# A new unit order for a Sinkhorn-sorted attention followed by a token-mixing MLP

## The chip, the cores and the metric

The kernel runs on one NeuronCore of a Trainium2 chip. The metric is the device time of one launch in microseconds (us), as the median of several runs. The engines are PE (matrix products, with its weight loads shown apart as PEld), VectorE (DVE), ScalarE (ACT), GpSimd (POOL) and SyncE (SP); each runs its own instructions in program order, and they meet through semaphores. Transfers (DMA) are started by GpSimd, SyncE or ScalarE.

## The reference

Four batches, eight heads, 768 tokens in eight blocks of 96, head size 64. Five Sinkhorn steps turn an 8x8 matrix per head into a nearly doubly stochastic P; P mixes the blocks of k and v; each block of q attends to its mixed block; the heads are joined to x (768 x 512 per batch), and a token-mixing MLP follows.

```python
for _ in range(5):
    P = exp(P - max(P, -1)); P = P / (sum(P, -1) + 1e-9); P = P / (sum(P, -2) + 1e-9)
k_sorted, v_sorted = einsum('bhij,bhjcd->bhicd', P, blocks of k), the same of v
attn = softmax(q_b @ k_sb.T / sqrt(64))          # per block of 96 tokens
x = (attn @ v_sb) joined over heads              # [4, 768, 512]
W_tok = (x @ w_q) @ (x @ w_k).T / sqrt(64)       # [768, 768] per batch
out = relu(W_tok @ x) @ w_out
```

## The kernel before

The work is cut into units, each a short function of a batch `b` and a number `n`. One table, `ORDER`, lists all 468 units, and the loop at the end issues them one after the other. Nothing else orders the work: an engine meets its instructions in the order in which their units stand in the table, and waits where a value or a buffer isn't ready. An item such as `K01:2` is unit `u_K` of batch 0, pair 1, with PSUM bank 2; `k01:A:2` is its copy out of that bank by engine A (ScalarE), D (VectorE), G (GpSimd) or S (SyncE, for transfers). Capital letters are PE work, apart from R, D and I, which are transfers.

What the units do, in the order of the data:

- `l..` loads. GpSimd starts the loads of k, v and q, each in two halves of four heads (`lk0a`, `lk0b`), with a cast from f32 to bf16 on the way (line L232; the MLP's weights L223 and L226). `I` brings the first batch's raw q by SyncE into the buffers XT (L268).
- `c` and `a` are the Sinkhorn steps, on VectorE and ScalarE in turn; they end with P's transpose (L197). `A` and `B` spread P over the partitions, `u` copies it to the tile PTR, and `n` builds the sorting matrices M (L253), for the first batch from PSUM, for the others from PTR.
- `Z` are idle products on the zero tile `fil`, `n` of them: nothing reads them.
- `z` (first batch) and `p` put a pair of heads of q side by side in a pair buffer; `z` casts from f32, `p` copies bf16 within SBUF. `Q` transposes the pair on PE, and `q` copies the result to QT.
- `K` and `Y` sort and turn k and v in one product against M, with copies `k`, `y` to KT. `F`, `f` turn the first batch's v back into VT; the other batches sort v with `V`, `v` into Vs, and six transfers `R` on SyncE (L330) bring it to VT.
- `S` scores, `e` exponential to E (L363), `P` weighted sum, `r` and `x` the division into X (L392).
- `T`, `t` transpose X on PE to XT for batches 0 and 1. For batches 2 and 3 the units `D` do it by two transposing transfers each on SyncE (L398).
- `J` projects to q and k of the MLP, `d` moves a half of it to other partitions (tile qD), `W`, `G`, `H` form the token mixing, `h` applies the relu, `O` multiplies by w_out, `o` copies to one of four output buffers `ot`, and `s` stores it (L485, for the last batch in parts at L488).

Every PE instruction stands on line L154; copies are on L158 (ScalarE), L160 (GpSimd) and L162 (VectorE). After the table a `guard` on GpSimd reduces the reciprocals (L500 and on) and branches to a slow path that isn't taken.

```python
    for item in ORDER.split():
        kind, arg = item[0], item.split(":")[1:]
        ...
        if kind.isupper() and kind not in "RNDI":
            fns[kind](b, n, int(arg[0]))
        else:
            fns[kind](b, n, arg[0], int(arg[1]) if len(arg) > 1 else None)
```

Of the kernel before, what the change touches and what calls it, by code (L numbers as in the profile page):

```python
# [19 lines left out]
ORDER = """  # L20
i00:G i02:D I00:S lk0b Z62:0 I01:S Z32:1 i03:G Z42:0 c00:D Z22:1 a01:A lk0a c01:D A00:0 Z52:1 lv0a
Z04:2 lv0b a02:A:0 c02:D lv1b Z12:0 lv1a z11:A lp z10:D a03:A Q01:0 c03:D Q00:1 q01:A:0 q00:A:1
a04:A c04:D z13:A lk1a z12:D a05:A Q03:1 c05:D q03:A:1 Q02:0 q02:A:0 lk1b B00:0 u00:A:0 n01:D:0
n10:G n03:D:0 K01:2 n02:D:0 Y01:4 n00:D:0 k01:A:2 lq1b K00:6 y01:A:4 S02:2 k00:D:6 n11:G Y02:0
e02:A:2 K02:4 y02:D:0 S01:6 lq1a e01:A:6 S00:2 F02:0 lo k02:A:4 F01:1 f02:D:0 Y00:6 e00:A:2 f01:D:1
S03:4 n20:G y00:D:6 K03:0 e03:A:4 V10:2 k03:D:0 lv2a F00:6 v10:A:2 V12:4 lk2a f00:D:6 S06:0 lv2b
R10:S S05:2 e06:A:0 v12:D:4 P01:6 e05:A:2 R11:S V11:0 lk2b r01:D:6 x01:D:6 R14:S K10:4 v11:A:0 K11:2
R15:S n30:G k11:A:2 S04:0 k10:D:4 R12:S P00:6 e04:A:0 R13:S K12:2 r00:D:6 x00:D:6 lq2a Y03:4 k12:A:2
P02:0 n21:G y03:A:4 r02:D:0 x02:D:0 T00:2 K13:6 t00:A:2 p12:G F03:4 p13:D T01:5 n31:G k13:A:6
f03:D:4 Q12:2 Q13:3 q12:D:2 P04:0 q13:A:3 P03:6 lq2b r04:D:0 x04:D:0 U00:4 S16:2 z01:A:4 r03:D:6  # L30
x03:D:6 S14:0 p10:G e16:A:2 U01:4 e14:A:0 S15:2 p11:G t01:D:5 T03:7 e15:A:2 z02:D:4 T02:6 t03:D:7
Q10:5 Q11:4 t02:A:6 q10:D:5 P13:2 lq3a q11:D:4 S10:0 r13:D:2 x13:D:2 S13:6 e10:A:0 S12:4 lv3b
e13:A:6 S11:0 J01:2 e12:A:4 J00:3 j01:D:2 lv3a P14:6 e11:A:0 j00:D:3 W01:2 d01:G P12:4 r14:D:6
x14:D:6 W00:2 d00:A P11:0 w00:A:2 r12:D:4 x12:D:4 lk3b K20:6 G00:2 k20:A:6 G01:2 r11:D:0 x11:D:0
T12:3 g00:A:2 T13:6 t12:A:3 lk3a V20:4 T11:7 t13:A:6 v20:D:4 H01:2 K21:0 h01:A:2 k21:D:0 lq3b R20:S
K23:4 K22:2 R21:S k23:D:4 V22:0 k22:A:2 O03:6 t11:D:7 v22:A:0 p21:G V21:2 o03:D:6 p20:G P10:4 R25:S
v21:A:2 Q21:0 r10:D:4 x10:D:4 R24:S H02:6 q21:A:0 p23:G H00:2 R23:S Q20:1 h02:A:6 p22:D R22:S T10:0
q20:D:1 Q22:4 Q23:5 t10:D:0 h00:A:2 S21:6 q23:D:5 J10:0 e21:A:6 q22:D:4 p31:G S20:2 j10:D:0 S23:4
e20:A:2 S26:6 p30:D J11:1 d10:G e26:A:6 Q30:0 j11:D:1 O00:2 e23:A:4 d11:D q30:D:0 W11:3 o00:A:2
S25:4 S24:0 e25:A:4 S22:6 O05:2 e24:A:0 O01:4 e22:A:6 P24:0 o01:D:4 O02:5 o05:A:2 r24:D:0 x24:D:0  # L40
s00:S P21:6 O04:2 o02:D:5 r21:D:6 x21:D:6 s01:S V30:0 o04:A:2 V32:4 v30:A:0 s02:S W10:3 Q31:2
v32:D:4 V31:6 w10:A:3 R30:S P23:0 v31:A:6 q31:D:2 R31:S K30:4 r23:D:0 x23:D:0 G10:3 R35:S k30:A:4
K31:6 G11:3 R32:S k31:A:6 K32:4 g10:D:3 R33:S P22:0 k32:A:4 p32:G S31:2 r22:D:0 x22:D:0 H12:6 R34:S
p33:G e31:A:2 H11:4 h12:A:6 h11:D:4 S32:2 D21:S Q32:0 Q33:1 e32:A:2 q32:D:0 H10:6 K33:4 q33:D:1
h10:A:6 S33:2 k33:D:4 P20:0 e33:A:2 O11:6 r20:D:0 x20:D:0 S34:2 o11:A:6 S35:4 O10:7 D20:S e35:A:4
P31:0 e34:A:2 o10:D:7 S36:4 O14:6 r31:D:0 x31:D:0 s10:G e36:A:4 P34:4 o14:A:6 P32:2 r34:D:4 x34:D:4
P33:0 S30:6 r33:D:0 x33:D:0 J21:4 e30:A:6 J20:5 j21:A:4 r32:D:2 x32:D:2 P30:0 j20:A:5 W21:4 W20:4
O12:5 d21:D w20:A:4 D31:S r30:D:0 x30:D:0 G20:4 o12:A:5 G21:4 d20:D D30:S O15:5 g20:A:4 H20:0
o15:D:5 H22:2 h20:A:0 H21:6 O13:4 s12:S h21:D:6 h22:A:2 O20:5 o13:D:4 O23:2 o20:A:5 s11:G J31:3
o23:D:2 J30:5 j31:D:3 O21:4 d31:D j30:A:5 d30:D W30:5 W31:5 o21:A:4 O25:3 w30:D:5 w31:A:5 s20:A  # L50
G31:2 o25:A:3 G30:2 O22:3 g30:A:2 H30:4 o22:D:3 H32:6 h30:A:4 H31:0 h32:D:6 O24:2 s21:S h31:A:0
O31:3 o24:D:2 O33:0 s22:S o31:A:3 s31:A O30:1 o33:D:0 O34:3 s33:S o30:D:1 O32:2 s30:S o34:D:3 O35:1
s34:S o32:A:2 s32:S o35:A:1 s35:S
"""


# [652 lines left out]
```

## Time and profile before

| | us |
|---|---|
| median of three runs | 102.31 |
| lowest and highest | 102.23, 105.89 |
| profiled execution | 102.0 |
| its span | 100.1 |
| PE busy | 86.0 |
| VectorE busy | 72.8 |
| ScalarE busy | 71.2 |
| GpSimd busy | 40.9 |

The span is the time between the first and the last instruction that the hardware profiler saw; the profiled execution took 1.9 us more than that. A row of the order of instructions reads: start, time, engine, line, operation, tile written and tiles read, shape, how many are merged, and in brackets how long the engine stood idle before and what ended it. Matrix products overlap one another, so the distance between two starts says more than the time beside them. The clock column is the share of its full speed that PE was granted.

### The profile page before, as it was taken

To read this page: it belongs to the slowest core of one execution; us is meant where nothing else is said; L and a number is where in the kernel's file an instruction comes from. 1 tells how busy PE (TensorE), PEld (TensorE's weight loads), DVE (VectorE), ACT (ScalarE), POOL (GpSimd) and SP (SyncE) were. 2 spreads that over 40 slices of the span, in tenths; PEclk is the share of its full clock that TensorE was granted. 3 is DMA by queue.
4 is the path that set the end of the run, shared out by engine and by line. 5 is a ranking of instruction groups with operands and counts; after the bars stand their busy time and mean duration, and the time that the engine had idled before them with its cause. 6 is when DMAs were issued, how large, how long until landed. Compare 5 with 4: busy or idle time off the path is not lost.

```text
span 100.1 us, 3190 instructions
## 1 busy us (share of the span) xinstructions
PE 86.0 (86%) x1332; PEld 59.6 (60%) x1332; DVE 72.8 (73%) x143; ACT 71.2 (71%) x100; POOL 40.9 (41%) x65
## 2 busy tenths in 40 slices
...
GB/s 14 278 342 219 203 203 203 200 203 202 219 248 248 212 202 205 202 209 197 227 236 248 214 269 416 263 98 194 58 184 131 181 220 229 110 213 213 360 354 124
DMA packets 24575, 21.39 MB, mean 214 GB/s; under 512 B 7280, under 2 KB 22640, under 8 KB 24560
## 3 DMA queue, kind: packets, MB, share of 16 engines
...
q14 instruction: 5, 0.04, 0.1%
...
## 4 chain that ended last, share of the span: by engine, by line
PE 51%; DMA 17%; DVE 14%; ACT 11%; issue 3%; SPq 0%; ACTq 0%; DVEq 0%
PE ps L154 51%; DMA VT<-Vs 8%; DMA XT<-X 5%; DMA XT<-in_q_dram 4%; DVE X L392 4%; ACT E L363 3%; ACT QT L158 2%; ACT Vs L158 2%; DVE Vs L162 1%; DVE mixT L462 1%; DVE QT L162 1%; DVE Rall L387 1%; DVE KT L162 1%; ACT Qn L158 1%; DVE VT L162 1%
## 5 line engine op out<-in xcount | busy, mean ns | idle before, releaser
L363 ACT ACTIVATE E<-ps 96x960 bf16<-96x960 f32 (+1 forms) x28 | 23.9, 900 | 2.7 <-PE ps L154 2.5
L154 PE MATMUL ps<-wo,mixT 128*128 128x512 bf16 x96 | 23.3, 380 | 0.0
L392 DVE TENSOR_TENSOR X<-ps,Rall 96x896 bf16<-96x896 f32 (+1 forms) x20 | 20.1, 1007 | 0.7
L162 DVE COPY ot<-ps 128x512 f32<-128x512 f32 x12 | 8.3, 690 | 10.6 <-PE ps L154 8.4
L154 PEld LDWEIGHTS <-mixT 128*128 128x128 bf16 x96 | 8.4, 98 | 9.0 <-issue 0.8
L158 ACT COPY ot<-ps 128x512 f32<-128x512 f32 (+1 forms) x13 | 7.6, 587 | 7.7 <-PE ps L154 7.1
L154 PEld LDWEIGHTS <-KT 64*128 64x128 bf16 (+1 forms) x288 | 8.8, 100 | 4.3 <-issue 3.0
L160 POOL COPY Qn<-Qn 128x768 bf16<-128x768 bf16 x9 | 7.3, 827 | 9.9 <-DMA Qn<-in_q_dram 9.9
L158 ACT CAST KT<-ps 128x768 bf16<-128x768 f32 x12 | 9.3, 800 | 2.5 <-PE ps L154 2.5
L154 PE MATMUL ps<-VT,E 96*128 96x65 bf16 x256 | 10.8, 193 | 0.3 <-DMA VT<-Vs 0.2
L154 PEld LDWEIGHTS <-E 96*128 96x128 bf16 x256 | 9.5, 97 | 2.2 <-issue 0.8
L154 PE MATMUL ps<-QT,KT 64*128 64x96 bf16 x256 | 9.5, 210 | 1.5 <-ACT E L363 1.1
L154 PE MATMUL ps<-idb,Qn 128*128 128x128 bf16 x96 | 7.5, 220 | 3.7 <-ACT Qn L158 2.2
L460 ACT ACTIVATE mixT<-ps 128x1024 bf16<-128x1024 f32 x9 | 8.9, 1025 | 1.8 <-PE ps L154 1.8
L154 PE MATMUL ps<-M,Kn 128*64 128x128 bf16 x192 | 9.2, 239 | 1.1 <-DVE M L253 0.9
L485 POOL DMA_DIRECT2D out_dram<-ot x2 | 1.1, 550 | 21.0 <-ACT E L363 10.7
L253 POOL TENSOR_TENSOR M<-PTR,m_p 128x512 bf16<-128x512 bf16 x6 | 7.9, 1309 | 2.7 <-PE ps L154 2.1
L154 PEld LDWEIGHTS <-Qn 128*128 128x128 bf16 x96 | 5.6, 98 | 5.1 <-ACT Qn L158 2.7
L162 DVE CAST KT<-ps 128x768 bf16<-128x768 f32 x8 | 7.4, 948 | 1.6 <-PE ps L154 1.6
L154 PEld LDWEIGHTS <-Kn 128*64 128x64 bf16 x192 | 7.2, 121 | 2.1 <-issue 1.6
L232 POOL DMA_DIRECT2D Kn<-in_k_dram x8 | 6.5, 818 | 2.7 <-DMA Kn<-in_k_dram 2.6
L154 PE MATMUL ps<-XT,wqk 128*128 128x384 bf16 x32 | 6.1, 327 | 1.0 <-DMA XT<-X 1.0
...
## 6 DMA issues: line engine op xcount, KB each, us to landing
Kn<-in_k_dram POOLq DMA_DIRECT2D x8, 384.0 KB, 14.5
...
```

The lines of the kernel that those rows point to most:

```text
L154: nc.tensor.matmul(o, w, x, is_transpose=t, start=start, stop=stop, skip_group_check=True)
L158: nc.scalar.copy(o, i)
L160: nc.gpsimd.tensor_copy(o, i)
L162: nc.vector.tensor_copy(o, i)
L232: nc.gpsimd.dma_start(out=t[x][:, h0:h1].rearrange("p h r d -> p h (r d)"), in_=src[b, h0:h1].rearrange("h (p r) d -> p h (r d)", p=P))
L253: ENG[e].tensor_tensor(out=M[b % 2][:, h0:h0 + hn], in0=src.unsqueeze(2).to_broadcast([P, hn, SP, NB]), in1=m_p.unsqueeze(1).unsqueeze(3). ...
L363: nc.scalar.activation(E[b % 2][:, n, 0:2 * w * BLK].rearrange("p (t a c) -> p a t c", a=2, c=BLK), PS[0:BLK, bank:bank + 2, 0:w * BLK].re ...
L387: nc.vector.reciprocal(Rall[:, b, n, :, 0:w], avps(bank, w)[:, :, :, D])
L392: nc.vector.tensor_mul(xo.rearrange("p (a t d) -> p a t d", a=2, d=D), avps(bank, w)[:, :, :, 0:D], Rall[:, b, n, :, 0:w].unsqueeze(3).to_ ...
L460: nc.scalar.activation(o, i, ACT.Relu)
L462: nc.vector.tensor_relu(o, i)
L485: ENG[e].dma_start(out=od[:, 2 * n:2 * n + 2, :], in_=oslot(b, 2 * n))
```

## The change

Only the table is replaced. The same 468 units stand in it, in another order, and for some the engine or the PSUM bank is another.

```diff
 ORDER = """
-i00:G i02:D I00:S lk0b Z62:0 I01:S Z32:1 i03:G Z42:0 c00:D Z22:1 a01:A lk0a c01:D A00:0 Z52:1 lv0a
...
+lk0a i02:D I01:S lv0a I00:S c00:D lk0b a01:A i00:G c01:D lv0b A00:0 lv1b a02:A:0 c02:D lv1a z13:A
+a03:A Q03:0 c03:D Z04:1 a04:A z12:A c04:D q03:A:0 Q02:1 a05:A Z42:0 z10:A c05:D Z52:2 Z22:0 z11:A
+Q00:2 q02:A:1 q00:D:2 B00:0 Q01:3 n01:D:0 Z32:2 n00:D:0 q01:A:3 Y01:4 n02:D:0 K01:6 u00:A:0 n03:D:0
...
```

The parts that the description names:

- Of the 16 idle products, before, eight stand ahead of everything on PE and eight right after `A`. Now four stand between the first and the second q transposes and six between the second and the third, all during the Sinkhorn steps, and three pairs come after P's product `B`: one before the first sort, one after the fifth, one between the sorts of the second batch's v.
- The pair copies `p` that VectorE made (three) are made by GpSimd and ScalarE; the casts `z` are all on ScalarE.
- The stores `s00`, `s01`, `s02` of the first batch stood on SyncE between two batches' `R` transfers. Now `s02` and `s00` follow the third batch's transposing transfers, and `s01` is on GpSimd; `s10` moved from GpSimd to SyncE. One `d` of the last batch became a transfer on SyncE.
- The first loads are issued ahead of the identity's build (`i00`), and the loads of the MLP's weights after those of the second batch.

VectorE at the end of the Sinkhorn steps. Before, from the last cast of raw q to the first copy of sorted k (Pm, tmp: the Sinkhorn matrix and its sums; PbT: P's transpose; M_107: the first batch's sorting matrices):

```order
L162 CAST Qn_70<-XT_92 128x2x6x64 [waits DMAHW2_49]
L188 TENSOR_REDUCE tmp<-Pm 32x8 [waits Activation_49]
L189 RECIPROCAL tmp<-tmp 32x8 [waits DVE_49]
L190 TENSOR_TENSOR Pm<-Pm,tmp 32x64 [waits DVE_49]
L193 TENSOR_REDUCE tmp<-Pm 32x8 [waits DVE_49]
L194 RECIPROCAL tmp<-tmp 32x8 [waits DVE_49]
L195 TENSOR_TENSOR Pb<-Pm,tmp 32x64 [waits DVE_49]
L197 STREAM_TRANSPOSE PbT<-Pb 32x64 [waits DVE_49]
L253 TENSOR_TENSOR M_107<-ps,m_p 128x256 [waits Activation_49]
L253 TENSOR_TENSOR M_107<-ps,m_p 128x256 x3
L162 CAST KT_82<-ps 128x768 [waits PE_49]
```

The same place now:

```order
L188 TENSOR_REDUCE tmp<-Pm 32x8 [waits Activation_49]
L189 RECIPROCAL tmp<-tmp 32x8 [waits DVE_49]
L190 TENSOR_TENSOR Pm<-Pm,tmp 32x64 [waits DVE_49]
L193 TENSOR_REDUCE tmp<-Pm 32x8 [waits DVE_49]
L194 RECIPROCAL tmp<-tmp 32x8 [waits DVE_49]
L195 TENSOR_TENSOR Pb<-Pm,tmp 32x64 [waits DVE_49]
L197 STREAM_TRANSPOSE PbT<-Pb 32x64 [waits DVE_49]
L162 COPY QT_80<-ps 128x768 [waits PE_49]
L253 TENSOR_TENSOR M_107<-ps,m_p 128x256 [waits PE_49]
L253 TENSOR_TENSOR M_107<-ps,m_p 128x256 x2
L253 TENSOR_TENSOR M_107<-ps,m_p 128x256 [waits Activation_49]
```

The cast is gone from ahead of the fifth step, a copy of transposed q (QT_80) stands between P's transpose and M, and three of the four M now wait for PE alone, the fourth for ScalarE.

GpSimd where the loads of the second and third batch meet the pair copies. Before, from the third batch's first load on (Kn, Vn, Qn: loads of k, v and q; Qn_70 <- Qn_69: the second batch's pair copies; Qn_71: the third batch's raw q):

```order
L232 DMA Vn_77<-in_v_dram 128x4x384
L232 DMA Kn_74<-in_k_dram 128x4x384
L232 DMA Vn_77<-in_v_dram 128x4x384
L232 DMA Kn_74<-in_k_dram 128x4x384
L253 TENSOR_TENSOR M_108<-PTR,m_p 128x512
L232 DMA Qn_71<-in_q_dram 128x4x384
L253 TENSOR_TENSOR M_107<-PTR,m_p 128x512
L160 COPY Qn_70<-Qn_69 128x2x6x64
L253 TENSOR_TENSOR M_108<-PTR,m_p 128x512
L232 DMA Qn_71<-in_q_dram 128x4x384
L160 COPY Qn_70<-Qn_69 128x2x6x64 x2
L232 DMA Qn_70<-in_q_dram 128x4x384
```

Now, from the second batch's last q load on:

```order
L232 DMA Qn_69<-in_q_dram 128x4x384
L253 TENSOR_TENSOR M_107<-PTR,m_p 128x512
L223 DMA ot_106<-in_moe_w_q_dram 128x256
L223 DMA ot_106<-in_moe_w_k_dram 128x256
L160 COPY Qn_70<-Qn_69 128x2x6x64 x3
L232 DMA Qn_71<-in_q_dram 128x4x384
L160 COPY Qn_70<-Qn_69 128x2x6x64
L232 DMA Kn_74<-in_k_dram 128x4x384
L232 DMA Vn_77<-in_v_dram 128x4x384 x2
L226 DMA wo<-in_moe_w_out_dram 128x4x512
L232 DMA Kn_74<-in_k_dram 128x4x384
```

The loads of the third batch's k and v (Vn_77, Kn_74) were issued ahead of every pair copy; now the third batch's first load, Qn_71, stands behind three pair copies, and its k and v behind all four.

SyncE from the third batch's `R` transfers to the last batch's transposing ones, as a piece of the difference (VT: sorted v; XT: transposed X; ot_103 to ot_106: the four output buffers):

```order
 L330 DMA VT_85<-Vs_84 16x8x528 x6
-L485 DMA out_dram<-ot_103 128x1024
-L485 DMA out_dram<-ot_104 128x1024
-L485 DMA out_dram<-ot_105 128x1024
 L330 DMA VT_86<-Vs_84 16x8x528 x6
 L398 DMA_TRANSPOSE XT_91<-X_89 128x16x96 x2
+L485 DMA out_dram<-ot_105 128x1024
+L485 DMA out_dram<-ot_103 128x1024
 L398 DMA_TRANSPOSE XT_92<-X_90 128x16x96 x2
+L485 DMA out_dram<-ot_106 128x1024
+L419 DMA qD_96<-qkT_94 64x384
 L485 DMA out_dram<-ot_104 128x1024
```

Three stores leave the place ahead of the last batch's `R` transfers; two of them stand between the two pairs of transposing transfers.

More of the change, by code (lines that the diff above doesn't have):

```diff
@@ L20 @@
 ORDER = """
-i00:G i02:D I00:S lk0b Z62:0 I01:S Z32:1 i03:G Z42:0 c00:D Z22:1 a01:A lk0a c01:D A00:0 Z52:1 lv0a
[L22 to L53, printed above, removed]
+lk0a i02:D I01:S lv0a I00:S c00:D lk0b a01:A i00:G c01:D lv0b A00:0 lv1b a02:A:0 c02:D lv1a z13:A
+a03:A Q03:0 c03:D Z04:1 a04:A z12:A c04:D q03:A:0 Q02:1 a05:A Z42:0 z10:A c05:D Z52:2 Z22:0 z11:A
@@ new lines @@
+Q00:2 q02:A:1 q00:D:2 B00:0 Q01:3 n01:D:0 Z32:2 n00:D:0 q01:A:3 Y01:4 n02:D:0 K01:6 u00:A:0 n03:D:0
+K02:2 y01:A:4 n10:G k01:D:6 K03:0 Y00:4 k03:A:0 k02:D:2 Z12:7 i03:G y00:A:4 S06:0 Y02:6 e06:A:0
+S02:4 lk1a y02:D:6 K00:2 e02:A:4 S03:0 n11:G k00:D:2 S04:6 e03:A:0 F00:4 F01:5 f00:D:4 lq1b e04:A:6
+S01:0 S00:2 lk1b F02:4 e01:A:0 V11:6 f02:D:4 lq1a e00:A:2 V10:0 f01:D:5 n20:G Z62:4 v10:A:0 v11:D:6
+V12:2 P01:4 v12:A:2 lp K11:0 r01:D:4 x01:D:4 Y03:6 k11:A:0 R14:S P00:2 p13:G y03:A:6 R15:S r00:D:2
@@ new lines @@
+x00:D:2 S05:4 P02:0 p12:G R10:S e05:A:4 Q13:6 F03:7 R11:S r02:D:0 x02:D:0 q13:A:6 K10:4 R13:S K12:2
+k10:A:4 Q12:6 R12:S f03:D:7 K13:0 k12:A:2 q12:D:6 P04:4 T01:7 k13:A:0 p11:G r04:D:4 x04:D:4 T00:6
+S16:2 lq2a S15:0 t01:D:7 e16:A:2 P03:4 t00:D:6 e15:A:0 p10:G U00:2 r03:D:4 x03:D:4 Q11:3 z01:A:2
+lk2a S14:6 Q10:0 e14:A:6 q11:D:3 U01:1 lv2a T02:4 q10:D:0 T03:5 t02:A:4 lv2b z02:D:1 S11:6 t03:D:5
+S13:2 e11:A:6 S10:0 lo P13:4 e10:A:0 lk2b J00:6 r13:D:4 x13:D:4 J01:7 lq2b e13:A:2 j00:D:6 P14:0
+j01:A:7 S12:4 r14:D:0 x14:D:0 P10:2 e12:A:4 d01:G W00:7 W01:7 r10:D:2 x10:D:2 lq3a K21:0 w00:A:7
@@ new lines @@
+P11:4 d00:G k21:A:0 P12:6 n21:G r11:D:4 x11:D:4 T13:2 p21:A K20:0 G01:3 k20:A:0 lv3b r12:D:6 x12:D:6
+G00:3 p20:G g00:A:3 V20:0 t13:D:2 V21:4 v20:A:0 n31:G V22:6 v21:D:4 T11:2 v22:A:6 T12:3 lv3a H01:0
+t12:D:3 R23:S H00:4 h01:A:0 Q21:6 n30:G h00:D:4 R25:S Q20:3 T10:7 t11:A:2 R21:S O03:0 q20:D:3 lk3a
+t10:A:7 R20:S q21:D:6 S20:2 H02:4 R22:S e20:A:2 S21:6 h02:D:4 O00:1 R24:S e21:A:6 K22:2 o00:D:1
+K23:4 p23:G o03:A:0 k22:D:2 S22:6 k23:A:4 J11:1 p22:G e22:A:6 J10:0 lk3b Q23:4 j11:A:1 Q22:5 lq3b
+q23:A:4 O05:6 q22:D:5 j10:D:0 p30:A p31:G S26:4 S25:2 d11:D S24:0 e26:A:4 O02:7 e24:A:0 S23:4
```

14 lines of the change are left out of this document (added).

## The prediction

> **What bounds the kernel now.** I read four views: the page's busy shares, the stretches of time, the order of instructions on each engine with what ended each idle gap, and the landings of single transfers. The first says that no engine is idle enough to be ignored.
>
> ```profile
> PE 86.0 (86%) x1332; PEld 59.6 (60%) x1332; DVE 72.8 (73%) x143; ACT 71.2 (71%) x100; POOL 40.9 (41%) x65
> ```
>
> The stretches show where that average breaks up. Columns: stretch, its length, busy time of PE, PEld, DVE, ACT and POOL with the number of instructions, the granted PE clock, the DMA share, GB/s.
>
> ```profile
> 8.00:9.00 1.00, 0.00 (x0) 0.00 (x0) 0.46 (x3) 0.95 (x3) 0.37 (x1) 1.00 1.30 212
> ...
> 11.00:12.00 1.00, 0.24 (x5) 0.07 (x2) 0.86 (x5) 0.90 (x2) 0.06 (x1) 0.67 1.32 203
> ...
> 17.00:18.00 1.00, 1.00 (x24) 0.83 (x22) 0.86 (x1) 0.33 (x1) 0.62 (x2) 0.50 1.33 205
> 18.00:19.00 1.00, 1.00 (x28) 0.92 (x23) 0.10 (x1) 0.70 (x1) 0.51 (x1) 0.92 1.30 205
> ...
> 20.00:25.00 5.00, 4.73 (x106) 4.11 (x106) 4.96 (x7) 4.93 (x7) 4.35 (x6) 1.00 1.32 203
> ...
> 30.00:35.00 5.00, 4.08 (x87) 3.31 (x88) 4.89 (x10) 3.31 (x5) 2.75 (x4) 1.00 1.23 230
> ```
>
> Three things. The clock is halved at about 11.3 us (0.67 over 11 to 12 means a third of that stretch at full) and comes back at about 18.2, while PE is full at half speed to 18. VectorE is full from 20 to 25 and from 30 to 35, ScalarE from 20 to 25: they empty PSUM. And DMA delivers an even 203 GB/s, so a queued load of 384 KB (393 kB) takes 1.9 us.
>
> PE's own order, with idle time before an entry and what ended it:
>
> ```profile
> 1.23 3.50 PE L154 MATMUL ps<-fil 128*128 128x512 bf16 x8 [1.23 <-DVE fil L206]
> ...
> 4.78 1.89 PE L154 MATMUL ps<-fil 128*128 128x512 bf16 x8
> ...
> 12.37 0.39 PE L154 MATMUL ps<-PbT,Lx 32*128 32x32 bf16 x8 [1.12 <-DVE PbT L197]
> 13.68 0.85 PE L154 MATMUL ps<-M,Kn 128*64 128x128 bf16 x12 [0.92 <-DVE M L253]
> ...
> 18.41 1.09 PE L154 MATMUL ps<-idb,KT 128*96 128x128 bf16 x16
> ...
> 20.00 0.39 PE L154 MATMUL ps<-QT,KT 64*128 64x96 bf16 x10
> 20.32 0.53 PE L154 MATMUL ps<-M,Kn 128*64 128x128 bf16 x12
> 20.87 0.61 PE L154 MATMUL ps<-Vn,M 128*128 128x128 bf16 x8
> ...
> 30.67 0.51 PE L154 MATMUL ps<-idb,Qn 128*128 128x128 bf16 x6 [0.94 <-DVE Qn L162]
> ...
> 49.74 0.83 PE L154 MATMUL ps<-idb,Qn 128*128 128x128 bf16 x12
> ...
> 75.20 1.47 PE L154 MATMUL ps<-XT,wqk 128*128 128x384 bf16 x8 [1.01 <-DMA XT<-X]
> ```
>
> Eight idle products took 3.50 us at the start (0.44 each) and 1.89 from 4.78 (0.24): PE was in truth at half speed to about 4.6, although the record prints 1.00 there. The warm clock was then spent: the long idle time follows, and the real work from 13.68 runs cold. Of the gaps after 20 us, two point to single causes, 0.94 and 1.01.
>
> **The change, part by part.** All sums are against the profiled execution: 100.1 us of span, 102.0 with what lies around it, 0.3 under the median of 102.31.
>
> *Clock.* From 13.68 to 18.41 PE makes five sorting groups of 12 and 30 score products: 4.73 us. At full clock a group takes 20.87 - 20.32 = 0.55 and ten scores 20.32 - 20.00 = 0.32, so 5 x 0.55 + 3 x 0.32 = 3.71: 1.0 less. Half of the 4.5 us at half clock, 2.25, is the other bound. That ScalarE waits for PE there is in its gaps, in the second and third row:
>
> ```profile
> 5.67 0.83 ACT L158 CAST Qn<-XT 128x768 bf16<-128x768 f32 x1 [0.54 <-DMA XT<-in_q_dram]
> ...
> 14.56 1.50 ACT L158 CAST KT<-ps 128x768 bf16<-128x768 f32 x2 [1.40 <-PE ps L154]
> ...
> 18.30 0.97 ACT L363 ACTIVATE E<-ps 96x960 bf16<-96x960 f32 x1 [0.97 <-PE ps L154]
> ```
>
> I take 1.5, between the bounds. It needs the clock back before 13.5. In the changed order PE starts with the first pair's q transposes, once ScalarE has cast the first raw q (5.67 + 0.83 = 6.5, first row), then four idle products, another pair, six more: dense from 6.5, but for some 0.4 us, through 12. Before, 3.4 us of dense work (1.23 to 4.6) brought the clock back, and 4.5 us (13.68 to 18.2) the second time; five are offered by 11.5.
>
> [...]
>
> *Head.* The casts of raw q leave VectorE's Sinkhorn chain, and the matrices M no longer wait for ScalarE's copy of P:
>
> ```profile
> 6.24 0.69 DVE L162 CAST Qn<-XT 128x768 bf16<-128x768 f32 x1
> ...
> 10.14 0.54 DVE L162 CAST Qn<-XT 128x768 bf16<-128x768 f32 x1
> ...
> 13.20 1.42 DVE L253 TENSOR_TENSOR M<-ps,m_p 128x256 bf16<-128x256 f32 x4 [0.89 <-ACT PTR L158]
> ...
> L162 DVE COPY QT<-ps 128x768 bf16<-128x768 bf16 x10 | 5.3, 550 | 0.1
> ...
> L158 ACT COPY QT<-ps 128x768 bf16<-128x768 bf16 x6 | 4.7, 796 | 1.4 <-PE ps L154 1.3
> ```
>
> Between 0 and all 1.23 of the casts stood in the chain; each ran beside a ScalarE step, so I take 0.3. P's product ends at 12.37 + 0.39 = 12.76 and M starts at 13.20: the copy of P took those 0.4. Against it, a q copy of 0.55 now stands on VectorE between P's transpose and M, a q copy of 0.8 stands on ScalarE ahead of the fifth exponential, and the product for P queues behind six idle products and a q transpose group. 0.7 gained, 0.55 and up to 0.7 lost: I count 0, from -0.4 to +0.7.
>
> *Idle products behind P.* Three pairs, six products, now stand among the sorting groups: 6 x 0.24 = 1.4 us. The first pair lies in PE's wait for M. The other two each wait until a PSUM bank is emptied, with scores and sorts queued behind them; if those would have waited for the same copies it costs nothing. I count +0.5, from 0 to 1.4.
>
> *Pair copies.* VectorE's three leave it; GpSimd gets two of them and gives one of its own to ScalarE, which takes two in all.
>
> ```profile
> 28.76 1.85 DVE L162 COPY Qn<-Qn 128x768 bf16<-128x768 bf16 x1
> 30.53 0.68 DVE L162 COPY VT<-ps 96x1024 bf16<-96x1024 bf16 x1
> ...
> 49.25 0.35 DVE L162 COPY Qn<-Qn 128x768 bf16<-128x768 bf16 x1
> ...
> L160 POOL COPY Qn<-Qn x9: 820/825/837, 28.3 to 61.0; 128x768 bf16<-128x768 bf16 x9
> ```
>
> The same copy takes 0.35 at 49 us and 1.85 at 28.8, in the middle of the full stretch; PE's 0.94 gap ends with it and the V copy queues behind. On GpSimd it takes 0.83. Gain: from 0.3 (only the 0.35 counts) over 0.94 to 1.5 (1.85 less 0.35); I take 1.2, since the V copy is late as well. ScalarE pays two copies later, at some 0.80 each by its q copies; behind PE's work there they are free, otherwise half of the 1.6 shows (second rival).
>
> *Transposing transfers.* The two of the third batch:
>
> ```profile
> L398 SPq DMA_TRANSPOSE XT<-X x1: 1667/1667/1667, 66.7 to 66.7; - x1
> ...
> DMA to landing us min/median/max: 3.6/3.6/3.6
> ...
> L398 SPq DMA_TRANSPOSE XT<-X x1: 1410/1410/1410, 70.2 to 70.2; - x1
> ...
> DMA to landing us min/median/max: 5.0/5.0/5.0
> ...
> 72.56 0.55 POOL L485 DMA_DIRECT2D out_dram<-ot  x1 [10.73 <-ACT E L363]
> ```
>
> The second is 1.4 us longer, a store was started beside it, and PE waited 1.01 for it at 75.20. Without the store I take 0.9 (0 to 1.0: if the store wasn't the cause nothing is gained). What is late next is the last weighted sum, which waits for ScalarE's last exponential and stands behind these projections on PE. The stores of the first batch now stand on SP behind these transfers, and the output copy that reuses their buffer waits on ScalarE with the copies for the next products behind it; by the distances above they land about when it is reached, so 0, or up to 0.8.
>
> Sum: -1.5 + 0 + 0.5 - 1.2 - 0.9 = -3.1. 102.0 - 3.1 = 98.9, and 0.3 to the median: **99.2**. Its own range, with a few of the bounds falling together, is 97.4 to 100.8. Products, copies and bytes stay the same in number, so nothing else is added or removed.
>
> **The rivals.**
>
> *Loads run dry (slower).* GpSimd issues every load in program order. In the new order the third batch's first load stands behind three pair copies, the last of which waits for the second batch's second q load; before, loads were issued long ahead.
>
> ```profile
> L232 POOL DMA_DIRECT2D Qn<-in_q_dram x1: 806/806/806, 16.6 to 16.6; - x1
> ...
> DMA to landing us min/median/max: 13.7/13.7/13.7
> ...
> L232 POOL DMA_DIRECT2D Qn<-in_q_dram x1: 806/806/806, 30.3 to 30.3; - x1
> ...
> DMA to landing us min/median/max: 15.5/15.5/15.5
> ...
> DMA to landing us min/median/max: 8.1/14.5/18.4
> ```
>
> That q load landed at 16.6 + 13.7 = 30.3. Copy 0.8, then an issue: a load to an almost empty queue took 8.1 (the shortest of the K loads), so 39.2, where an unbroken queue would land one at 32.2: dry for 7.0. The third batch's last q load then lands at 30.3 + 15.5 + 7.0 = 52.8, its pair copy ends at 53.6, and the transposes that needed it at 49.74 are 3.9 late. 102.0 + 3.9 - 0.9 + 0.3 = 105.3. It decides once the queue is dry for over 4 us: then those transposes come 45.8 + 4 + 0.8 - 49.74 = 0.9 late, which eats the gain of the transposing transfers. Against it: the 8.1 was taken at the start, beside both raw q transfers; and the first load now starts ahead of the identity's build and two weight loads move behind that q load, which I therefore expect some 2 us earlier, with a dry time of 0 to 2. Chance 0.12.
>
> *The copying engines hold it (same).* From 20 to 25 us VectorE has 0.04 us of slack and ScalarE 0.07; sorts that come earlier wait for the same copies. Then the clock's 1.5 is lost and ScalarE's extra copies show: -1.2 - 0.9 + 0.5 + 0.8 = -0.8, 101.5. For it: 4.96 and 4.93 of 5.00. Against it: the gaps of 1.40 and 0.97 show both had room before 20. Chance 0.18.
>
> *The clock comes late (same).* The idle products run at 0.44 in place of 0.24, P's product is 0.7 late, and the sorts stay cold: -3.1 + 1.5 + 0.7 = -0.9, 101.4. [...] Chance 0.12.
>
> That the change doesn't do what it says is mostly excluded by the order; only a store that ScalarE issues may run beside the last transposing transfer, for which the 1.4 above is the bound.
>
> **How the numbers follow.** Forecast 0.58, then 0.18, 0.12 and 0.12. A measurement of this kernel tells about 2% (2.05 us) from no change: faster means below 100.26. Of the forecast 0.55 lies there: faster 0.55. Same: 0.18 + 0.12 and 0.03 of the forecast, 0.33. Slower 0.12. The range leaves out the slower rival and some 0.06 below: from 97.3 to 102.5, which takes in the two rivals near 101.5 with a microsecond of unknown costs.
>
> **What would show it.** Clock: granted 1.00 from 12 us on, sorting groups 0.55 apart from the first; else the third rival. Head: first sort between 13.3 and 14.4. Pair copies: none on VectorE, no 0.9 gap of PE near 30, VT copies not delayed. Transposes: each 3.6, no PE gap ahead of the third batch's first projection. Loads: DMA share over 1.2 without a break between 28 and 34 us; a hole of over 4 us there proves the first rival. I am wrong if PE starts the sorts warm and yet reaches the last 28 output products less than 2 us earlier.

## The result: slower, 110.55 us

The changed kernel takes 110.55 us (median; 109.76 to 111.44), the kernel before on the same chip 102.41. The ratio is 1.078, with a 95% interval from 1.064 to 1.091. The profiled execution took 109.76, with a span of 107.9 where it had 100.1. Some executions run at a lower granted clock (of before, beside kernel 16, 0.927 to 0.935 in place of 0.966) and take up to some 4 us longer (there 104.69 to 106.30 in place of 102.15); ratios and the times compared below are of the others, called comparable.

The page of the changed kernel, busy time of the engines, shows the same work in a longer time:

```profile
PE 85.5 (79%) x1320; PEld 59.5 (55%) x1332; DVE 71.7 (66%) x137; ACT 72.2 (67%) x104; POOL 42.3 (39%) x68
```

Where the time lies is in PE's order of instructions. These are the changed kernel's first sort, its wait for the MLP's weights, the sorts of the fourth batch's v, the first weighted sums of the fourth batch, the two projections behind the transposing transfers, and the last output products:

```profile
13.93 0.53 PE L154 MATMUL ps<-M,Vn 128*64 128x128 bf16 x12
...
31.59 0.24 PE L154 MATMUL ps<-idb,ot 128*64 128x128 bf16 x1 [0.89 <-DMA ot<-in_moe_w_q_dram]
32.18 0.41 PE L154 MATMUL ps<-idb,ot 128*64 128x128 bf16 x7 [0.34 <-DMA ot<-in_moe_w_k_dram]
...
59.89 1.06 PE L154 MATMUL ps<-Vn,M 128*128 128x128 bf16 x16
...
66.12 0.81 PE L154 MATMUL ps<-wo,mixT 128*128 128x512 bf16 x3 [0.16 <-DVE Rall L387]
...
71.71 0.59 PE L154 MATMUL ps<-VT,E 96*128 96x65 bf16 x14 [2.57 <-DMA VT<-Vs]
...
77.56 1.46 PE L154 MATMUL ps<-XT,wqk 128*128 128x384 bf16 x8
...
86.81 1.48 PE L154 MATMUL ps<-XT,wqk 128*128 128x384 bf16 x8 [0.99 <-DMA XT<-X]
...
93.16 6.23 PE L154 MATMUL ps<-wo,mixT 128*128 128x512 bf16 x27
```

The same places of the kernel before that are not in the prediction:

```profile
59.57 1.06 PE L154 MATMUL ps<-Vn,M 128*128 128x128 bf16 x16
...
71.00 0.60 PE L154 MATMUL ps<-VT,E 96*128 96x65 bf16 x14
...
90.16 6.22 PE L154 MATMUL ps<-wo,mixT 128*128 128x512 bf16 x28
```

At the sorts of the fourth batch's v the two are nearly level (59.89 and 59.57): of the gains of the forecast nothing is left there. At the last output products the changed kernel is 3.0 behind (93.16 - 90.16), 2.7 of it lost since those sorts. But the span is 7.8 longer. The other 4.8 lie behind the last product: from 102 on no engine of the changed kernel is busy and next to nothing is transferred (columns as in the prediction; the second fence is the kernel before):

```profile
100.00:102.00 2.00, 0.00 (x0) 0.00 (x0) 0.00 (x0) 0.01 (x1) 0.00 (x0) 1.00 0.85 324
102.00:104.00 2.00, 0.00 (x0) 0.00 (x0) 0.00 (x0) 0.00 (x0) 0.00 (x0) 1.00 0.00 0
104.00:106.00 2.00, 0.00 (x0) 0.00 (x0) 0.00 (x0) 0.00 (x0) 0.00 (x0) 0.56 0.01 4
...
```

```profile
98.00:100.10 2.10, 0.00 (x0) 0.00 (x0) 0.00 (x0) 0.00 (x0) 0.00 (x0) 1.00 0.26 100
```

The DMA share falls to 0.00 at 102, and the kernel ends at 107.9. What was still running is GpSimd's own program. Its order in the changed kernel, the last store and the guard (first and last of its seven steps):

```profile
95.11 0.53 POOL L485 DMA_DIRECT2D out_dram<-ot  x1 [2.60 <-ACT ot L158]
95.65 0.75 POOL L500 CROSS_LANE_REDUCE s<-Rall 96x1 f32<-96x280 f32 x1
...
99.18 0.18 POOL L506 TENSOR_SCALAR flag<-s 1x1 int32<-1x1 f32 x1
```

and the instructions of its queue behind the guard, by source line (count, duration in ns as min/median/max, first and last start in us), in the changed kernel:

```profile
L675 POOLq EVENT_SEMAPHORE  x5: 17/42/43, 103.4 to 103.7; - x5
L675 POOLq COMPARE_BRANCH  x1: 45/45/45, 100.3 to 100.3; - x1
...
L704 POOLq DRAIN  x3: 46/101/2437, 104.6 to 107.6; - x3
```

The same two views of the kernel before:

```profile
83.36 0.55 POOL L485 DMA_DIRECT2D out_dram<-ot  x1 [10.24 <-DVE ot L162]
...
L675 POOLq EVENT_SEMAPHORE  x5: 17/43/43, 91.1 to 91.5; - x5
L675 POOLq COMPARE_BRANCH  x1: 45/45/45, 88.5 to 88.5; - x1
...
L704 POOLq DRAIN  x3: 46/101/2273, 92.3 to 99.8; - x3
```

The guard takes 3.5 from its first step to its last; from the branch that leaves the slow path out it is 2.6 before the change and 3.1 after it to the next instruction shown of that queue, and an instruction that the profile calls DRAIN takes 2.3 and 2.4. All of it stands behind GpSimd's last store. Before, that store was issued at 83.36 and all of it ran beside the output products. The new table gives GpSimd three stores of the third batch, the last at 95.11, and the chain ends 12 us later, at 107. These are the units 20, 21 and 22; 20 stood on ScalarE, 21 and 22 on SyncE. The list of parts in the section on the change leaves them out.

### The profile page after: what moved, and what is told of

Its sections match the earlier page's. It is cut to its first block, busy times and chain, and to the rows that moved or that the text cites. A ratio compares the mean times of both kernels' runs of the same rounds, so it can differ in the third digit from the quotient of the medians.

```text
span 107.9 us, 3182 instructions
## 1 busy us (share of the span) xinstructions
PE 85.5 (79%) x1320; PEld 59.5 (55%) x1332; DVE 71.7 (66%) x137; ACT 72.2 (67%) x104; POOL 42.3 (39%) x68
## 4 chain that ended last, share of the span: by engine, by line
DMA 35%; PE 28%; POOL 8%; ACT 7%; DVE 6%; issue 6%; SPq 3%; ACTq 0%; DVEq 0%; POOLq 0%
PE ps L154 28%; DMA Qn<-in_q_dram 13%; DMA ot<-in_moe_w_k_dram 8%; DMA XT<-X 5%; DMA XT<-in_q_dram 4%; DMA VT<-Vs 4%; POOL M L253 4%; ACT E L363 3%; SPq L330 2%; DVE X L392 2%; ACT Qn L158 1%; POOL Kn L232 1%; POOL Qn L232 1%; ACT ot L158 1%; DVE M L253 1%
## 5 line engine op out<-in xcount | busy, mean ns | idle before, releaser
L154 PE MATMUL ps<-wo,mixT 128*128 128x512 bf16 x87 | 22.3, 380 | 0.7 <-DVE Rall L387 0.2
L485 POOL DMA_DIRECT2D out_dram<-ot x4 | 2.2, 539 | 26.6 <-ACT ot L158 25.8
L158 ACT CAST KT<-ps 128x768 bf16<-128x768 f32 x14 | 10.8, 810 | 1.2 <-PE ps L154 1.2
L154 PE MATMUL ps<-idb,Qn 128*128 128x128 bf16 x96 | 8.7, 242 | 2.5 <-ACT Qn L158 1.9
L154 PEld LDWEIGHTS <-Qn 128*128 128x128 bf16 x96 | 6.5, 108 | 4.9 <-ACT Qn L158 3.1
L462 DVE TENSOR_SCALAR mixT<-ps 128x1024 bf16<-128x1024 f32 x7 | 8.4, 1218 | 0.4 <-PE ps L154 0.4
L162 DVE COPY QT<-ps 128x768 bf16<-128x768 bf16 x9 | 4.9, 554 | 4.6 <-PE ps L154 4.5
L154 PE MATMUL ps<-M,Kn 128*64 128x128 bf16 x192 | 7.6, 222 | 0.1
L387 DVE RECIPROCAL Rall<-ps 96x14 f32<-96x14 f32 (+1 forms) x20 | 4.6, 231 | 3.7 <-PE ps L154 2.6
L154 PEld LDWEIGHTS <-Kn 128*64 128x64 bf16 x192 | 5.9, 110 | 1.7 <-issue 1.3
```

The source lines that it names most:

```text
L154: nc.tensor.matmul(o, w, x, is_transpose=t, start=start, stop=stop, skip_group_check=True)
L158: nc.scalar.copy(o, i)
L162: nc.vector.tensor_copy(o, i)
L387: nc.vector.reciprocal(Rall[:, b, n, :, 0:w], avps(bank, w)[:, :, :, D])
L462: nc.vector.tensor_relu(o, i)
L485: ENG[e].dma_start(out=od[:, 2 * n:2 * n + 2, :], in_=oslot(b, 2 * n))
```

## The experiments

Units are written as in the table. In the kernels that begin from the changed kernel "stores back" always means the three edits of the first experiment, "transfer order" that of the eighth.

**1. The three stores off GpSimd.** From the changed kernel:

```diff
-s20:G ... s22:G ... s21:G
+s20:A ... s22:S ... s21:S
```

> The changed kernel with its three stores of the third batch taken off GpSimd (20 to ScalarE, 21 and 22 to SyncE), nothing else. Tail theory: GpSimd's closing part (the guard's seven steps, the branch, the drain) can only start behind its last store, 95.1 in the changed kernel, and takes 12.1 us from that issue to its end; without these stores it runs beside the output products and the span ends about 3.1 us after the last output copy, as before: 110.5 - 4.8 = 105.7. Rival (the late loads hold everything and the quiet end is only what a late end looks like): within 1 us of 110.5.

Measured: ratio to before 1.028 (1.010 to 1.045), where the changed kernel has 1.078; the comparable times are 104.19 and 105.17. Its profile, of an execution of 107.8, shows the closing part of GpSimd done early and the end of the span, 106.0, 3.0 behind the last output copy:

```profile
102.45 0.59 ACT L158 COPY ot<-ps 128x512 f32<-128x512 f32 x1 [0.28 <-PE ps L154]
...
L704 POOLq DRAIN  x3: 46/101/2196, 92.9 to 105.7; - x3
```

The tail theory holds: some 5 us for the engine of three stores (0.050 of 102, about 2 us either way).

**2. One store onto GpSimd, in the kernel before.**

```diff
-s22:S
+s22:G
```

> The kernel before with one single store, 22, moved from SyncE to GpSimd, nothing else. Tail theory: that store is issued at 92.0, and GpSimd ends 12.1 us later at 104.1, the span 0.8 later at 104.9 in place of 100.1: 107.1 in place of 102.3, with all output copies where they were. Rival: one store's engine changes nothing, 102.3, since GpSimd is idle there.

Measured: one comparable time, 106.16, where before took 101.5 to 102.5 on the same chip: 3.7 to 4.6 more. Its profile shows the store and the last output copy; the span ends at 104.0:

```profile
91.60 0.53 POOL L485 DMA_DIRECT2D out_dram<-ot  x1 [8.76 <-DVE ot L162]
...
95.74 0.58 ACT L158 COPY ot<-ps 128x512 f32<-128x512 f32 x1 [0.28 <-PE ps L154]
...
L704 POOLq DRAIN  x3: 46/101/2355, 100.8 to 103.7; - x3
```

The last copy ends at 96.3, 0.7 earlier than in the profile of before (97.0, from the row below), and yet the kernel ends 7.7 later than that copy in place of 3.1. The long drain ends 11.6 behind GpSimd's last store here (100.8 + 2.4 - 91.6), 11.2 before and 11.9 in the changed kernel.

```profile
96.41 0.59 ACT L158 COPY ot<-ps 128x512 f32<-128x512 f32 x1 [0.28 <-PE ps L154]
```

**3 and 4. The loads in about the order of before**, in the changed kernel (3) and with the stores back as well (4):

```diff
-... lv1a z13 ... n10 ... i03 ... lk1a ... n11 ... lq1b ... lk1b ... lq1a ... n20 ... lp ... p13 ... p12 ... p11 ... lq2a ...
+... lv1a lp i03 lk1a lk1b z13 ... n10 lq1b ... n11 lq1a lo ... n20 lv2a lk2a lv2b lk2b lq2a ... p13 lq2b ... p12 ... p11 ...
```

> The changed kernel with GpSimd's loads issued early, in about the order they have before the change (the MLP weights and the second batch's K ahead of the first matrix M, the third batch's loads ahead of the pair copies); stores and every other unit as in the changed kernel. Loads theory: PE's waits of 0.89 and 0.34 for the MLP weights at 31.6 go, and the halved clock of 32.6 to 36.0 with them (1.7), and the 2.57 for the V transfers at 71.7 as far as it comes from the late third and fourth batches; the last output product comes 3 to 5 us earlier and, with the late stores still on GpSimd, the whole 106 to 107.5. Rival (the loads are hidden anyway, the stage losses come from the copies and the transposing transfers): last output product within 1 us of 99.2, whole 109.5 to 111.

> Both edits: loads early and the three stores off GpSimd. If the tail and the loads are all that makes the changed kernel slower, what is left is the gain that was forecast from the clock, the pair copies and the transposing transfers: 99 to 101. If the new order loses elsewhere too, 102 to 104. If neither edit matters, 110.5.

Measured: 1.069 (1.048 to 1.089) and 1.027 (1.019 to 1.036): neither differs from the same kernel with its loads late (1.078 and 1.028). The waits for the weights are gone, and others stand in their place, here in kernel 3 (a profile of 110.8; that of kernel 4 has 2.11 and 2.00 at the same two places):

```profile
27.82 0.51 PE L154 MATMUL ps<-idb,Qn 128*128 128x128 bf16 x6 [2.05 <-POOL Qn L160]
...
43.97 0.83 ACT L158 COPY Qn<-Qn 128x768 bf16<-128x768 bf16 x1 [3.14 <-DMA Qn<-in_q_dram]
...
45.55 1.97 PE L154 MATMUL ps<-Vn,M 128*128 128x128 bf16 x24 [2.91 <-ACT KT L158]
```

The first is a pair copy that waits for q's load, and in the second ScalarE has waited 3.14 for another one with the copy to KT behind it. The new order of units wants q's loads sooner than the load order of before brings them, so the loads theory in that form falls. With stores back, 104.7 is left, not the 99 to 101 that was expected: another cause remained.

**5. The idle products alone**, in the kernel before: six behind the first q transposes, six at the others, four behind P's product.

```diff
-... lk0b Z62:0 I01:S Z32:1 i03:G Z42:0 c00:D Z22:1 ... Z52:1 ... Z04:2 ... Z12:0
+... Q00:1 Z04:2 Z62:2 ... Q03:1 Z42:2 Z12:2 ... Q02:0 Z52:3 ... B00:0 Z22:5 Z32:5
```

> The kernel before with nothing changed but where its sixteen idle products stand: six behind the first pairs' q transposes, six between and behind the other q transposes, four behind the product for P, none at the start. Clock theory (term of the forecast, 1.0 to 2.25, taken 1.5): the granted clock is full by 13, the first sorting groups are 0.55 apart, the whole is 1.5 shorter, 100.9. Rival (the copying engines hold it): the sorts start warm, but ScalarE and VectorE, full from 20 to 25, take the gain back: 102.0 to 102.4. A cold spell later on, as in the changed kernel, would be no part of this run, as the loads are those of before.

Measured: 0.994 (0.990 to 0.998), a gain of 0.6 us (0.2 to 1.1). Sorts run at full clock from the first (granted 1.00 from 13 to 18, and 0.53 for the first group where before has 0.85); what takes the rest is in two rows:

```profile
14.00 0.53 PE L154 MATMUL ps<-M,Kn 128*64 128x128 bf16 x12
...
20.73 0.61 PE L154 MATMUL ps<-Vn,M 128*128 128x128 bf16 x8 [0.97 <-DMA Vn<-in_v_dram]
```

The first sort begins 0.3 later than before (13.68), and the sorts of the second batch's v wait 0.97 for its load. Before, they began at 20.87, when that load had just landed (at 20.5).

**6 and 12. The pair copies**, in the kernel before, all four (6) and copy 13 alone (12):

```diff
-p13:D ... p21:G ... p22:D ... p30:D
+p13:G ... p21:A ... p22:G ... p30:A
```

> The kernel before with four pair copies on the engines that have them after the change: 13 and 22 from VectorE to GpSimd, 30 from VectorE and 21 from GpSimd to ScalarE; order and everything else as before. Pair theory (term of the forecast, 0.3 to 1.5, taken 1.2): PE's 0.94 at 30.67 and VectorE's 1.85 copy go, 101.1. Rival: GpSimd's queue, with loads behind its copies, or ScalarE's two copies cost it again: 102.3 or more.

> The kernel before with pair copy 13 alone moved from VectorE to GpSimd. The kernel before with all four moved took 1.0125. Theory: copy 13 is the gain that was forecast (PE's 0.94 at 30.67), at 0.995, and the 1.25 per cent loss and more came from copies 21 and 30 on ScalarE and 22 behind 23 on GpSimd. Rival: GpSimd's loads behind copy 13 cost it, 1.00 to 1.01.

Measured: 1.0125 (1.006 to 1.019) for all four, 0.997 (0.986 to 1.008) for copy 13 alone. The start of the sorts differs between these executions (13.68, 14.11 and 14.45), though the edit doesn't touch what stands ahead of them, and so does the end of the cold stretch: near 18.2 by the granted clock before, and later in kernels 6 and 12, where the 16 transposes behind the score products, begun at 19.02 and 19.36, take 1.17 and 1.35 to the next product, in place of 1.03 from 18.41. The distance from the score products just behind both to a late step (the token mixing of the last batch) says more. The rows are of before, kernel 6 and kernel 12:

```profile
25.11 0.39 PE L154 MATMUL ps<-QT,KT 64*128 64x96 bf16 x10 [0.31 <-ACT Vs L158]
...
87.43 1.06 PE L154 MATMUL ps<-X,wk 96*64 96x256 bf16 x16 [0.16 <-ACT wk L158]
```

```profile
25.68 0.39 PE L154 MATMUL ps<-QT,KT 64*128 64x96 bf16 x10 [0.17 <-ACT Vs L158]
...
30.66 0.51 PE L154 MATMUL ps<-idb,Qn 128*128 128x128 bf16 x6 [0.25 <-POOL Qn L160]
...
88.25 1.06 PE L154 MATMUL ps<-X,wk 96*64 96x256 bf16 x16 [0.16 <-ACT wk L158]
```

```profile
26.20 0.39 PE L154 MATMUL ps<-QT,KT 64*128 64x96 bf16 x10 [0.17 <-ACT Vs L158]
...
87.67 1.06 PE L154 MATMUL ps<-X,wk 96*64 96x256 bf16 x16 [0.16 <-ACT wk L158]
```

Before: 87.43 - 25.11 = 62.32. Copy 13 alone: 61.47, a gain of some 0.85. All four: 62.57, so the other three cost some 1.1. These are single profiles; the times alone don't tell copy 13 from no change. PE's gap of 0.94 did shrink to 0.25. That copies 21 and 30 on ScalarE and 22 on GpSimd cost more than 13 gains is shown in sum; which of the three it is stays open.

**7. The store beside the transposing transfer, later in the table**, in the kernel before:

```diff
-... D20:S P31:0 e34:A:2 ... s10:G ... J21:4 ... J20:5
+... D20:S P31:0 e34:A:2 ... J21:4 ... J20:5 s10:G
```

> The kernel before with its store 10 moved in GpSimd's order to where the third batch's projections stand, so that it no longer starts beside the transposing transfer of 70.2. Store theory (term of the forecast, 0 to 1.0, taken 0.9): that transfer lands in 3.6 in place of 5.0, PE's wait of 1.01 at 75.20 goes, 101.4. Rival: the transfer's length has another cause (what else moves then), the wait stays: 102.3.

Measured: two comparable times, 101.95 and 102.15, where before has 101.6 to 102.2 beside them: the same. But the edit didn't move the store in time. No unit of GpSimd stands between its old place and its new one, so GpSimd's own order is unchanged, and it issues the store at 72.71, where before has 72.56:

```profile
72.71 0.55 POOL L485 DMA_DIRECT2D out_dram<-ot  x1 [10.93 <-ACT E L363]
```

The transfer landed after 4.7 in place of 5.0, and PE's wait is 0.70 in place of 1.01; kernels 6 and 12, which leave this store alone, have 4.7 with waits of 0.71 and 0.77. So the store theory was not tested. In before and in kernels 5, 6, 7 and 12 the transfer beside which this store starts takes 4.7 to 5.1 and the other three 3.5 to 3.8, which speaks for the theory; but in kernel 8 the last of the four takes 3.8, although ScalarE starts a store 1.9 behind its start. The cause stays open.

**8. The V transfers in the order of their copies.** The six transfers of the fourth batch wait for three copies into Vs: 30 and 31 for copy 30, 32 and 33 for copy 31, 34 and 35 for copy 32. The changed kernel makes copy 32 last and queues transfer 35 first on SyncE. From the changed kernel, stores back as well:

```diff
-R35:S ... R34:S ... R31:S ... R33:S ... R32:S ... R30:S
+R33:S ... R32:S ... R30:S ... R31:S ... R34:S ... R35:S
```

> The changed kernel with the three stores off GpSimd and the six V transfers of the fourth batch on SyncE in the order in which their copies are made (33, 32, 30, 31, 34, 35; in the changed kernel the first, 35, waits for the last of three V copies and the other five stand behind it); loads as in the changed kernel. Transfer-order theory: the first is issued near 61.7 in place of 63.0, the last lands 1.7 earlier, PE's wait of 2.57 at 71.7 falls to 0.9 and the whole by 1.5 against the changed kernel with its stores moved alone (104.7 where the runs are least disturbed): 103.2. Rival (the transfers are slow because of what runs beside them, not late): the wait stays above 2, 104.7.

Measured: 100.90 us, ratio 0.990 (0.984 to 0.996): faster than both kernels. SyncE's six transfers in the kernel before, the changed one, and this one:

```profile
61.30 5.34 SPq L330 DMA_DIRECT2D VT<-Vs  x6
```

```profile
63.01 4.71 SPq L330 DMA_DIRECT2D VT<-Vs  x6
```

```profile
61.42 4.08 SPq L330 DMA_DIRECT2D VT<-Vs  x6
```

and PE in this kernel:

```profile
66.09 0.81 PE L154 MATMUL ps<-wo,mixT 128*128 128x512 bf16 x3 [0.16 <-issue]
...
69.28 0.59 PE L154 MATMUL ps<-VT,E 96*128 96x65 bf16 x14 [0.17 <-issue]
...
83.74 1.46 PE L154 MATMUL ps<-XT,wqk 128*128 128x384 bf16 x8
```

PE comes to the same products at 66.09 and, in the changed kernel, at 66.12: up to there the late loads and the cold stretch of the changed kernel had cost nothing against this one. Then it has no wait for the V transfers in place of 2.57, which leaves it 2.4 ahead at the weighted sums (69.28 against 71.71) and 3.1 ahead at the fourth batch's projections (83.74 against 86.81, where the wait of 0.99 is gone too). The expectation had 1.5 for this; the measured step from the first experiment is 0.038 of 102, 3.9, about 2 either way.

**9. Transfer order alone**, stores left on GpSimd:

> The changed kernel with the V transfers of the fourth batch in the order of their copies, stores left on GpSimd. If the two causes add up: the changed kernel stands at 1.078 of before and at 1.028 with its stores moved, and at 0.990 with both edits, so the transfer order alone should take 0.038 off: 1.040, with the last output copy near 96.5 and the quiet end of some 8 us still there. If the guard hides what the transfers give (GpSimd ends a fixed time behind its last store, and that store moves with the products), the same 1.040; if the late store itself slows the transfers, above 1.06.

Measured: 1.046 (1.033 to 1.058). Its profile has the last store on GpSimd at 92.36 and the last output copy ending at 97.3, and ends at 105.1, 7.8 behind that copy. The two causes add up within the intervals: 0.050 for the stores alone, 0.032 for the transfer order alone, 0.088 for both.

```profile
92.36 0.53 POOL L485 DMA_DIRECT2D out_dram<-ot  x1 [2.61 <-ACT ot L158]
...
96.67 0.58 ACT L158 COPY ot<-ps 128x512 f32<-128x512 f32 x1 [0.28 <-PE ps L154]
```

**14 and 16. A late transfer order in the kernel before.** In 14 transfer 33 got ahead of the copy that it reads in the table, so this kernel sends the third batch's v in its place, and the copy waited for the transfer (PE waits 2.51 behind it). It answers another question than the one put. 16 has the transfer behind the copy and sends the fourth batch's v.

```diff
-V31:6 ... R30:S ... v31:A:6 ... R31:S ... R35:S ... R32:S ... R33:S ... R34:S
+V31:6 ... v31:A:6 R33:S ... R32:S ... R31:S ... R35:S ... R34:S ... R30:S
```

> The kernel before with the V transfers of the fourth batch in an order in which the first two wait for the last of the three V copies (33, 32, 31, 35, 34, 30), as in the changed kernel. If an order like that costs whatever else stands there: 1.5 to 4 us, 103.5 to 106. If it costs because the changed kernel also has PE at the fourth batch's first weighted sums at 69 in place of 72.6: the transfers land near 70 here, PE comes at 72.6, and the two transposing transfers queued behind them are at most 0.5 later: 102.0 to 102.5.

> The kernel before with the V transfers of the fourth batch in an order in which the first two, 33 and 32, wait for the last of its three V copies (33, 32, 31, 35, 34, 30), and the first stands behind that copy; in the run before this one it stood ahead of the copy, so that the copy waited for the transfer instead. If such an order costs whatever else stands there: 1.5 to 4 us more than before. If it costs in the changed kernel because PE also comes to the fourth batch's first weighted sums at 69 in place of 72.6: the transfers land near 70 here, PE comes at 72.6, and the two transposing transfers behind them are at most 0.5 later: the same as before, within 0.5 us.

14 has no comparable time beside before. Measured for 16: 101.63, 101.78 and 101.78, where before has 102.15 beside them. A late order costs nothing there. By the order of units PE's first weighted sums of the fourth batch are those at 71.00 before the change; the expectations took 72.60, where the next three groups begin. Behind the sorts of v, in the kernel before, the last transfer lands 8.9 (68.5 - 59.57) and PE comes to these sums 11.4 (71.00 - 59.57). In the profile of kernel 16, an execution of 105.95, it is 10.0 (73.6 - 63.59) and 11.5 (75.07 - 63.59, the row below), and PE doesn't wait. In the changed kernel it is 11.6 (67.12 + 4.35 - 59.89, by the second row, of its chain of waits), and PE would have come 9.3 behind the sorts (71.71 - 2.57 - 59.89). So what the order costs depends on the place of the reader, which is some 2 us nearer in the changed kernel: with 16's landing its wait would be 0.7 (10.0 - 9.3). Why the last transfer lands another 1.6 later there, though the first starts 3.1 behind the sorts in both (63.01 - 59.89, 66.71 - 63.59), stays open.

```profile
75.07 0.60 PE L154 MATMUL ps<-VT,E 96*128 96x65 bf16 x14
```

```profile
67.12 4.35 DMA VT<-Vs
```

**10, 11 and 13. Past the repairs.** From kernel 8: the loads a little earlier (10), pair copy 30 back on VectorE (11: `p30:A` becomes `p30:D`), and 10 with the second and third batch's transfers in the order of their copies (13).

```diff
-... n10:G ... i03:G ... lk1a ... n20:G ... lp ... p13:G ... p12:G ... p11:G ... lq2a ... p10:G ... lk2a ... lv2a ... lv2b
+... i03:G lk1a ... n10:G ... n20:G ... lp lq2a lk2a ... p13:G ... p12:G lv2a ... p11:G ... p10:G lv2b
 ...
-R14:S ... R15:S ... R10:S ... R11:S ... R13:S ... R12:S ... R23:S ... R25:S ... R21:S ... R20:S ... R22:S ... R24:S
+R10:S ... R11:S ... R13:S ... R12:S ... R14:S ... R15:S ... R20:S ... R21:S ... R23:S ... R22:S ... R25:S ... R24:S
```

> Both repairs (stores off GpSimd, transfer order) and the loads a little earlier on GpSimd: the second batch's first K load ahead of its first matrix M, the third batch's first q and K loads ahead of the four pair copies, its V loads between them. Loads theory: PE's waits of 1.34 for K at 40.2, 0.35 for V at 44.1 and 0.20 for the MLP weights at 31.6 go, 1.5 to 1.9 shorter than with both repairs alone (100.9): 99.0 to 99.4. Rival (a load moved ahead only moves the wait to another load, as with the whole order of before): 100.5 to 101.5.

> Both repairs, and pair copy 30 back on VectorE as before the change. If ScalarE's copy of 54.5 (0.83, with three exponentials queued behind it) is on the path there, as the 0.96 that the kernel before lost between 48 and 67 with its pair copies moved would say: 100.2 to 100.5 against 100.9. If not: 100.9.

> The kernel with both repairs and nudged loads, and the V transfers of the second and third batch in the order of their copies as well (10, 11, 13, 12, 14, 15 and 20, 21, 23, 22, 25, 24; the changed kernel starts with 14, which waits for the last copy, and with 23, which waits for the second). Order theory: PE's wait of 1.96 for V transfers at 35.7 falls under 0.8, the whole by up to 1.2 against 0.978 of before: 0.966 to 0.972. Rival (they are late by the DMA queue, which is full there, not by the order on SyncE): the wait stays, 0.975 to 0.98.

Measured: 10 has 0.978 (0.957 to 0.998), with comparable times of 99.80 and 100.25; 11 has 0.988 (0.975 to 1.002), not told apart from 8; 13 has a median of 99.53 (98.97 to 100.72). Before took 104.1 and more beside 13, none of it comparable, so the ratio there (0.946) says too much; against the 101.6 to 102.2 that before took beside the other kernels it stands near 0.976, an estimate across chips. In the second batch the profile of 10, an execution of 101.86, has a wait of 1.96 for V transfers at 35.74, and that of 13 none there. That the transfer order causes it is not shown: 8, with the same order and later loads, doesn't have it either.

13 is the fastest kernel of this study; between it and 10 no run on the same chip decides.

## Why the prediction was wrong

It forecast 99.2 and a range to 102.5; the time is 110.55. No rival had either cause.

**The step that failed first** is the sentence "Products, copies and bytes stay the same in number, so nothing else is added or removed". The stores did not change in number, but three of them moved to GpSimd, and what is queued behind GpSimd's last store is the kernel's closing part. The prediction followed the first batch's stores to SyncE and to the buffers that they free, and counted 0 to 0.8; it doesn't speak of the third batch's, and didn't ask what stands behind a store on GpSimd. The rows to see it were in the trace of before: 83.36 for the last store, 92.3 + 2.3 = 94.6 for the end of the drain, 11.2 apart, against a last output copy that ends at 97.0. With a store at 95.11 in place of 83.36 that chain ends behind everything else. It measured 5.1 us alone (1.078 - 1.028 of 102), and 5.7 between kernels 9 and 8 (1.046 - 0.990).

**The second** is the fourth batch's V transfers, which the prediction doesn't mention; PE's longest wait for such a transfer before was 0.18. The one that needs the last copy was queued first, and their reader moved forward by some 2 us (11.4 to 9.3 behind the sorts); together 3.9 us with the stores back, 3.2 with them on GpSimd. The forecast put both at nothing.

**Clock.** The mechanism was right: sorts at full clock from the first (at 13.93, in the predicted 13.3 to 14.4; 0.53 for the first group where before has 0.85), so the third rival didn't happen. The record prints 1.00 from the start here too; the durations put the return near 12.2, later than the 11.5 of the prediction's count (the six idle products from 9.92 still take 2.51, the six transposes from 12.26 take 0.50 where those from 9.23 took 0.82). Whether the ten idle products alone brought it back or the transposes among them helped, no run tells apart. In kernel 5 the warm clock is worth 0.6 (0.2 to 1.1), not 1.5: the term was mis-sized, because what came next, the sorts of the second batch's v, waited 0.97 for that batch's load. The rows of the changed kernel show the clock, and one thing not foreseen, a second stretch at half speed behind PE's wait for the weights. It begins at about 32.6:

```profile
17.00:18.00 1.00, 1.00 (x33) 0.83 (x32) 0.57 (x1) 0.91 (x3) 0.98 (x4) 1.00 1.33 207
...
30.00:33.00 3.00, 1.77 (x35) 1.34 (x30) 2.13 (x4) 1.71 (x3) 2.41 (x4) 0.93 0.82 162
33.00:36.00 3.00, 3.00 (x39) 2.66 (x37) 1.45 (x3) 1.47 (x3) 3.00 (x5) 0.51 1.09 147
```

**Head and idle products.** The first sort came 0.25 later (13.93 against 13.68), inside the bounds of 0.4 gained to 0.7 lost. (Those bounds don't follow from the prediction's own terms, which add up to between 1.1 gained and 0.85 lost.) The three pairs behind P were not tried apart.

**Pair copies.** Sign wrong in sum. VectorE lost its three copies and PE's gap of 0.94 closed to 0.25, as forecast, but copy 13 alone is worth some 0.85 and not 1.2: a part goes to PE's next wait for ScalarE's exponentials, 0.63 in place of 0.43 near 37 us. The two copies that ScalarE takes were called free behind PE's work there; with copy 22 they cost some 1.1, more than copy 13 brings. The second rival (the copying engines hold it) had this right, at a price of 0.8.

**Transposing transfers.** The term of 0.9 was not tested, as kernel 7 left the store where it was in time. What the prediction made of it for the changed kernel failed: the four took 5.7, 5.8, 3.5 and 5.6, not 3.6 each. The new table starts stores just ahead of the first (66.89, on GpSimd), beside the second (72.72, on SyncE) and beside the fourth (82.79, on ScalarE); for this last store the prediction gave 1.4 as the bound, and 5.6 is 2.0 more than 3.6. There is no gap ahead of the third batch's first projection, as forecast, and one of 0.99 ahead of the fourth's, which went when the V transfers came in order.

**Loads run dry.** The first rival's mechanism is there: the DMA share is 0.82 between 30 and 33, PE waited 0.89 and 0.34 for the weights, and the fourth batch's last pair copies came at 65.4 where they came at 60.2. But the repaired kernel, with the same loads, is level with the changed one at 66 and beats before, so this isn't why the change is slower. Loads a little earlier seem to bring another 1%, but the intervals overlap.

"I am wrong if PE starts the sorts warm and yet reaches the last 28 output products less than 2 us earlier" came true: it reached them 3.0 later. What the new table does without its two faults is kernel 8: 1.0 us faster (0.4 to 1.7), a third of the forecast gain of 3.1.
